# Splitting one 1280 KB weight load into four loads of 32 partitions, with another destination

## The chip, the cores and the metric

The kernel runs on one core of a Trainium2 chip. The metric is the device time of one execution in microseconds (us); the median of three runs stands for a kernel. All data is fp32.

## The reference, cut to what matters

The program is one decoder block for two sequences (B = 2) with one new token each (D = 512): a layer norm, attention over a long cache, a gated MLP beside it, and a residual.

```python
xn = _layernorm(x, axis=-1)                      # x: [2, 1, 512]
q = (xn @ wq)                                    # wq: [512, 4096] -> 32 heads of 128
scores = einsum("bhqd,bhkd->bhqk", q, k) * Dh**-0.5   # k_cache: [2, 8, 32768, 128]
o = einsum("bhqk,bhkd->bhqd", softmax(scores), v)     # v_cache: the same shape, 4 heads share a kv head
s = o @ wo                                       # wo: [4096, 512]
gate, up = xn @ W_gate, xn @ W_up                # [512, 1792] each
g = silu(((gate * (gate > 0)) * up) @ W_down)    # W_down: [1792, 512]
return x + s * g
```

The caches are 2 x 268 MB, the weights 28 MB together. Nearly all bytes are read once.

## The kernel before

**The ring.** All large data goes through three slots of 64 KB per partition (16384 floats, `slot`, L66): first wq in slot one, W_gate and W_up in slot two, W_down in slot three, then 64 tiles of k and v, then wo. A slot is loaded again once everything that reads it is done. All these loads are issued by SyncE through one helper (`load`, L69 and L70), so that every one of them has line 70 in the profile; they wait in one queue and the sixteen DMA engines take their packets from it in order, each engine at its own pace.

**wq.** A partition p of slot one holds four rows of wq, 4p to 4p + 3, of 4096 floats each: 64 KB, the whole slot. The load is in two parts. The first (128 x 13824 floats, 6912 KB, 55296 bytes per partition) brings all but the first 2560 floats (10 KB, `SHIFT`) of each partition and starts at the slot's beginning. The second brings those 128 pieces of 10 KB to the slot's end. Its source is written with an outer dimension of eight (`"(t a i) n -> i a t n"`, a = 8, t = 16): the piece of row group 8t + a goes to partition 16a + t, so that the pieces stand in another order of partitions than the rest of wq. The left operand of the products follows: `xnp` has four planes of the normalized x, one for each i, and a fifth plane (L170 to L177) in the order of the moved pieces.

**What follows, in the order of the code.** W_gate and W_up (3584 KB each, 28672 bytes per partition), W_down (3584 KB), then the k and v tiles (8192 KB each, 65536 bytes per partition).

**project_q (L180).** q for both sequences: eight column blocks of 512, four to a half; a half is sixteen matmuls of 128 x 512 (four row steps i by four blocks c, each block to its own 32 partitions of the result, L194). A product whose columns were moved reads the fifth plane. q is then turned into the form that the scores need (L203 to L227). `mlp_gu` (L238), `mlp_h` and `mlp_down` (L264) compute the MLP. The first k tile can be loaded when project_q has read slot one, the second when mlp_gu has read slot two, the first v tile when mlp_down has read slot three.

**The loop.** For each of sixteen pairs of sequence and kv head: two k tiles and two v tiles are loaded; VectorE transposes the k tile in place in blocks (L304), TensorE computes the scores (L315), the softmax follows (L344 to L382), TensorE multiplies with v (L391). At the end come wo in six pieces, the output product, and four small stores.

Of the kernel before, what the change touches and what calls it, by code (L numbers as in the profile page):

```python
# [8 lines left out]
F32 = mybir.dt.float32  # L9
# [4 lines left out]
P = 128  # L14
Q = 32
# [7 lines left out]
SHIFT = 2560  # L23
# [5 lines left out]
def kernel(  # L29
# [12 lines left out]
    nc = tc.nc  # L42
    B, HKV, SK, DH = kc.shape
    D = x.shape[2]
# [5 lines left out]
    NKC = D // P  # L50
    FC = F // 4
    FI = F // P
# [6 lines left out]
    const = ctx.enter_context(tc.tile_pool(name="const", bufs=1))  # L59
# [3 lines left out]
    SLOT = ROWS * DH  # L63
    KT, VT, PT = {}, {}, {}

    def slot(name):  # L66
        return ring.tile([P, SLOT], F32, tag="r", align_bytes=ALIGN, name=name)

    def load(dst, src):  # L69
        nc.sync.dma_start(dst, src)  # L70

    wqs = slot("wq")
    QN = wq.shape[1]
    load(wqs[:, : SLOT - SHIFT], wq.rearrange("(p i) n -> p (i n)", p=P)[:, SHIFT:])
    load(
        wqs[:, SLOT - SHIFT :],
        wq.rearrange("(t a i) n -> i a t n", a=8, i=NKC)[0, :, :, :SHIFT],
    )

    row = work.tile([P, 512], F32, tag="row", name="xp", bufs=3)  # L80
    xp = row[:32, :]
# [2 lines left out]
    nc.vector.memset(xy, 0.0)  # L84
    nc.scalar.dma_start(xp[:B, :], x.rearrange("b s d -> (b s) d"))

    gus = slot("gu")
    gut = gus[:, : 2 * NKC * F].rearrange("p (w i f) -> p w i f", w=2, i=NKC)
    for w, src in enumerate((wg, wu)):
        load(  # L90
            gus[:, w * NKC * F : (w + 1) * NKC * F],
            src.rearrange("(p i) f -> p (i f)", p=P),
        )
    wds = slot("wd")
    load(wds[:, : FI * D], wd.rearrange("(p i) d -> p (i d)", p=P))
    wdt = wds[:, : FI * D].rearrange("p (i d) -> p i d", i=FI)

    ident = const.tile([P, P], F32, name="ident")
# [8 lines left out]
    n = 1  # L107
# [5 lines left out]
    for s in range(NS):  # L113
# [39 lines left out]
    m_ps = ps_c.tile([P, 512], F32, name="m_ps")  # L153
# [6 lines left out]
    xc, sq = xc_row[:32, :], sq_row[:32, :]  # L160
# [5 lines left out]
    nc.scalar.activation(st[:, 3:4], st[:, 2:3], AF.Sqrt, bias=eps_t, scale=1.0 / D)  # L166
    nc.vector.reciprocal(st[:, 4:5], st[:, 3:4])
    nc.vector.tensor_scalar(xc, xc, st[:, 4:5], None, op0=ALU.mult)
    xnp = const.tile([P, NKC + 1, 32], F32, name="xnp")
    nc.vector.tensor_copy(  # L170
        sq[:, :P].rearrange("b (a t) -> b a t", a=8),
        xc.rearrange("b (t a i) -> b i a t", a=8, i=NKC)[:, 0],
    )
    xcol = xc.rearrange("b (p i) -> b i p", i=NKC)
    for i in range(NKC):
        nc.tensor.transpose(m_ps[:, i * 32 : (i + 1) * 32], xcol[:, i, :], ident[:32, :32])  # L176
    nc.tensor.transpose(m_ps[:, NKC * 32 : (NKC + 1) * 32], sq[:, :P], ident[:32, :32])  # L177
    nc.vector.tensor_copy(xnp.rearrange("p k m -> p (k m)"), m_ps[:, : (NKC + 1) * 32])

    def project_q():  # L180
        pick = ident.rearrange("p (c m) -> p c m", c=4)[:, :, :B]
        nq = 2 * REP * 4 * B
        spread = work.tile([P, 4, 4, Q], F32, tag="row", name="spread", bufs=3)
        for kb in range(4):
            nc.vector.tensor_copy(  # L185
                spread[:, :, kb, :], ident.rearrange("p (e l) -> p e l", e=4)
            )
        for half in range(2):
            pq = S[0][half]
            for i in range(NKC):  # L190
                for c in range(4):
                    n0 = (half * 4 + c) * 512
                    lo = i * QN + n0 - SHIFT
                    nc.tensor.matmul(  # L194
                        pq[32 * c : 32 * c + 32, :],
                        xnp[:, i if lo >= 0 else NKC, :],
                        wqs[:, lo % SLOT : lo % SLOT + 512],
                        start=(i == 0),
                        stop=(i == NKC - 1),
                    )  # L200
        for half in range(2):
            qs = work.tile([P, 512], F32, tag="row", name=f"qs_{half}", bufs=3)
            nc.vector.tensor_copy(qs, S[0][half])  # L203
            for h in range(REP):
                lo = (half * REP + h) * 4 * B
                nc.tensor.matmul(
                    m_ps[:, lo : lo + 4 * B],
                    qs[:, h * DH : (h + 1) * DH],
                    pick,
                    start=True,  # L210
                    stop=True,
                )
        turned = const.tile([P, nq], F32, name="turned")
        nc.vector.tensor_copy(turned, m_ps[:, :nq])
        for e in range(4):
            nc.tensor.matmul(
                pt_ps[:, e * nq : (e + 1) * nq],
                spread[:, e].rearrange("p k l -> p (k l)"),
                turned,
                start=True,  # L220
                stop=True,
            )
        qp = pt_ps[:, : 4 * nq].rearrange("p (e f h m) -> p f m e h", e=4, f=2, h=REP)
        for half in range(2):
            for kb in range(4):
                part = slice(Q * kb, Q * kb + Q)
                nc.vector.tensor_copy(  # L227
                    qt[part, half * 8 : half * 8 + 8, :, kb * REP : (kb + 1) * REP],
                    qp[part, half],
                )  # L230
# [168 lines left out]
    def finish_group(g):  # L399
# [11 lines left out]
        if b == B - 1:  # L411
            src = OS.pop(hk).rearrange("p b c (q i) -> p q (b c) i", q=4)
            for dq in range(4):
# [7 lines left out]
                )  # L421

    project_q()
    mlp_gu(0)
    mlp_gu(1)
# [3 lines left out]
    with tc.manual_schedule(engines=None):  # L429
# [23 lines left out]
        g, h = NG - 2, NG - 1  # L453
# [23 lines left out]
        i = 0  # L477
# [22 lines left out]
        for i in range(WO_WIDE):  # L500
            a = i % 4
# [4 lines left out]
                start=(i < 4),  # L506
                stop=(i >= WO_WIDE - 4),
# [4 lines left out]
        for c in range(4):  # L512
# [4 lines left out]
                start=False,  # L517
                stop=False,
# [40 lines left out]
```

## Time and profile before

| | |
|---|---|
| time, median of 3 runs (lowest to highest) | 1330.22 us (1328.72 to 1330.5) |
| time of the profiled execution | 1328.65 us |
| span of the profiled execution, first to last instruction | 1326.8 us |
| busy: PE / DVE / ACT | 839.5 / 677.2 / 49.5 us |
| read from memory | 564.67 MB, 426 GB/s over the span |

The page gives busy time by engine, the span in 40 equal slices with what the DMA engines moved in each, the queues, the chain of work that ended last, and the groups of instructions. DMA packets are counted where they start, so the rate of a short stretch scatters with how many large packets start in it; the share is the mean busy share of the sixteen DMA engines. Times inside the trace are us from the span's start.

### The profile page before, as it was taken

To read this page: it belongs to the slowest core of one execution; us is meant where nothing else is said; L and a number is where in the kernel's file an instruction comes from. 1 tells how busy PE (TensorE), PEld (TensorE's weight loads), DVE (VectorE), ACT (ScalarE), POOL (GpSimd) and SP (SyncE) were. 2 spreads that over 40 slices of the span, in tenths; PEclk is the share of its full clock that TensorE was granted. 3 is DMA by queue.
4 is the path that set the end of the run, shared out by engine and by line. 5 is a ranking of instruction groups with operands and counts; after the bars stand their busy time and mean duration, and the time that the engine had idled before them with its cause. 6 is when DMAs were issued, how large, how long until landed. Compare 5 with 4: busy or idle time off the path is not lost.

```text
span 1326.8 us, 10365 instructions
## 1 busy us (share of the span) xinstructions
PE 839.5 (63%) x4657; PEld 206.5 (16%) x4657; DVE 677.2 (51%) x574; ACT 49.5 (4%) x133; POOL 0.7 (0%) x6
## 2 busy tenths in 40 slices
PE   0746577574656757565685746677576657756775
PEld 0201112120111212111121201112021111201121
DVE  2256291835629183562918447291745719178620
ACT  0000000000000000000000000000000000000000
POOL 0000000000000000000000000000000000000000
PEclk9979789788979879787987969888887878978899
DMA  9999999999999999999999999999999999999997
GB/s 289 423 426 441 429 441 424 439 433 431 433 429 441 429 437 429 443 427 433 433 437 427 437 437 427 435 433 439 427 435 433 435 431 433 435 435 435 422 426 310
DMA packets 11016, 565.33 MB, mean 426 GB/s; under 512 B 1226, under 2 KB 1242, under 8 KB 1628
## 3 DMA queue, kind: packets, MB, share of 16 engines
q1 hardware_dynamic: 10944, 564.67, 99.2%
q8 instruction: 36, 0.59, 0.2%
q14 instruction: 8, 0.07, 0.0%
q10 hardware_dynamic: 28, 0.01, 0.0%
HBM read 564.67 MB, written 0.00 MB: 426 GB/s over the span
## 4 chain that ended last, share of the span: by engine, by line
DMA 52%; DVE 24%; PE 22%; issue 2%; ACT 0%; another core or an unknown queue 0%; ACTq 0%; SPq 0%; DVEq 0%
DMA k<-in_A_k_cache_dram 41%; DVE k L304 19%; PE o_ps L391 8%; DMA v<-in_A_v_cache_dram 6%; PE pt_ps L370 6%; PE s L315 5%; DMA wo<-in_A_wo_dram 3%; DMA wq<-in_A_wq_dram 3%; DVE mx L328 2%; DVE pt L374 2%; PE s L194 1%; PE s L238 1%; DVE mrow L354 0%; PE m_ps L378 0%; PE m_ps L357 0%
## 5 line engine op out<-in xcount | busy, mean ns | idle before, releaser
L315 PE MATMUL s<-k,qt 128*32 128x512 f32 x2048 | 460.0, 693 | 342.0 <-DVE k L304 341.9
L304 DVE STREAM_TRANSPOSE k<-k 128x2048 f32<-128x2048 f32 x256 | 567.0, 2279 | 169.8 <-DMA k<-in_A_k_cache_dram 163.0
L391 PE MATMUL o_ps<-v,pt 128*16 128x512 f32 x2048 | 229.9, 604 | 15.0 <-DMA v<-in_A_v_cache_dram 14.9
L315 PEld LDWEIGHTS s<-k,qt 128*32 128x32 f32 x2048 | 87.7, 122 | 710.0 <-DVE k L304 563.5
L403 DVE SCALAR_TENSOR_TENSOR os<-o_ps,rl,mask 128x512 f32<-128x512 f32 x16 | 12.0, 750 | 226.1 <-PE o_ps L391 226.1
L370 PE MATMUL pt_ps<-w,perm 128*128 128x512 f32 x128 | 84.7, 796 | 32.3 <-ACT w L367 17.9
L367 ACT ACTIVATE w<-s,nb 128x512 f32<-128x512 f32 x64 | 43.2, 686 | 1163.0 <-DVE nb L361 1160.9
L391 PEld LDWEIGHTS o_ps<-v,pt 128*16 128x16 f32 x2048 | 58.2, 98 | 171.5 <-issue 151.7
L328 DVE TENSOR_REDUCE mx<-s 128x1 f32<-128x512 f32 x64 | 42.7, 667 | 66.4 <-PE s L315 66.4
L374 DVE STREAM_TRANSPOSE pt<-pt_ps 128x512 f32<-128x512 f32 x32 | 22.9, 717 | 98.6 <-PE pt_ps L370 98.6
L370 PEld LDWEIGHTS pt_ps<-w,perm 128*128 128x128 f32 x128 | 26.9, 233 | 73.1 <-ACT w L367 39.1
L194 PE MATMUL s<-wq,xnp 128*32 128x512 f32 x64 | 8.7, 704 | 20.8 <-DMA wq<-in_A_wq_dram 20.8
L415 PE MATMUL ot_ps<-os,place 128*128 128x256 f32 x64 | 16.0, 392 | 7.0 <-DVE os L403 7.0
L203 DVE COPY qs<-s 128x512 f32<-128x512 f32 x2 | 1.4, 693 | 28.6 <-PE s L194 28.6
L378 PE MATMUL m_ps<-l,same 128*128 128x1 f32 x32 | 6.3, 267 | 13.5 <-DVE l L377 13.5
L345 PE MATMUL m_ps<-ident,m 128*1 128x128 f32 x16 | 4.3, 270 | 15.5 <-DVE m L344 15.5
L415 PEld LDWEIGHTS ot_ps<-os,place 128*128 128x128 f32 x64 | 11.5, 189 | 15.6 <-DVE os L403 14.4
L357 PE MATMUL m_ps<-negs,mrow 1*128 1x1 f32 x32 | 6.0, 256 | 11.7 <-DVE mrow L354 11.7
L367 ACT ACTIVATION_READ_ACCUMULATOR w<-s,nb 128x1 f32 x64 | 12.8, 201 | 0.0
L176 PE MATMUL m_ps<-ident,xc 32*128 32x32 f32 x4 | 0.7, 298 | 15.0 <-DVE spread L185 15.0
L378 PEld LDWEIGHTS m_ps<-l,same 128*128 128x128 f32 x32 | 5.0, 195 | 32.0 <-DVE l L377 32.0
L264 PE MATMUL m_ps<-wd,ht 128*32 128x512 f32 x28 | 6.3, 1006 | 5.3 <-DMA wd<-in_B_W_down_dram 5.3
(75 smaller groups left out, 81.7 us busy)
## 6 DMA issues: line engine op xcount, KB each, us to landing
v<-in_A_v_cache_dram SPq DMA_DIRECT2D x2, 4096.0 KB
wq<-in_A_wq_dram SPq DMA_DIRECT2D x1, 6912.0 KB, 19.9
wo<-in_A_wo_dram SPq DMA_DIRECT2D x1, 4096.0 KB
gu<-in_B_W_gate_dram SPq DMA_DIRECT2D x1, 3584.0 KB
gu<-in_B_W_up_dram SPq DMA_DIRECT2D x1, 3584.0 KB
wd<-in_B_W_down_dram SPq DMA_DIRECT2D x1, 3584.0 KB, 58.5
wo<-in_A_wo_dram SPq DMA_DIRECT2D x1, 2048.0 KB
wq<-in_A_wq_dram SPq DMA_DIRECT2D x1, 1280.0 KB
```

Source lines behind the costliest of these rows:

```text
L194: nc.tensor.matmul(pq[32 * c : 32 * c + 32, :], xnp[:, i if lo >= 0 else NKC, :], wqs[:, lo % SLOT : lo % SLOT + 512], start=(i == 0), sto ...
L238: nc.tensor.matmul(ps[32 * c : 32 * c + 32, :FC], xnp[:, i, :], gut[:, w, i, c * FC : (c + 1) * FC], start=(i == 0), stop=(i == NKC - 1),)
L304: nc.vector.transpose(KT[t][:, part], KT[t][:, part])
L315: nc.tensor.matmul(S[u][s][Q * c : Q * c + Q, :], qt[:, g, e, :], mov[:, s, c, e], start=(e == 0), stop=(e == 3),)
L328: nc.vector.reduce_max(MX[g][:, i : i + 1], S[u][s], axis=AX.X)
L367: nc.scalar.activation(w, S[u][s], AF.Exp, bias=nb, scale=SCALE, accum_out=LS[g][:, i : i + 1])
L370: nc.tensor.matmul(pt_ps, perm[:, s, :], w, start=(s == 0), stop=(s == NS - 1))
L374: nc.vector.transpose(pt.rearrange("p j m -> p (j m)"), pt_ps)
L378: nc.tensor.matmul(m_ps[:, 300:301], same.rearrange("p r h -> p (r h)"), l, start=True, stop=True)
L391: nc.tensor.matmul(o_ps[Q * a : Q * a + NC * REP], w[:, j, s * NC * REP : (s + 1) * NC * REP], v[:, s, j], start=(u == 0 and s == 0 and j ...
L403: nc.vector.scalar_tensor_tensor(OS[hk][:, b], o_ps, RL.pop(g), mask.unsqueeze(2).to_broadcast([P, NC, DH]), op0=ALU.mult, op1=ALU.mult,)
L415: nc.tensor.matmul(ot_ps.rearrange("p b c i -> p (b c) i"), place[:, lo : lo + P], src[:, dq], start=(hk == 0 and dq == 0), stop=(hk == HK ...
```

## The change

The 128 pieces of 10 KB are loaded by four loads of 32 partitions instead of one load of 128. The order in which the pieces are read is unchanged: load h has an outer dimension of eight (a) and an inner one of four (b), and reads row groups 32h + 8b + a; with 4h + b for t, that is 8t + a as before, for each a in the same order. What differs is where they are written. Loads 0 and 1 write partitions 0 to 31 and 32 to 63 of slot one's last 10 KB, loads 2 and 3 the same partitions of 10 KB in slot three behind W_down, which had been unused; a takes four consecutive partitions in each load. Partitions 64 to 127 get none.

The products follow: where one matmul over 128 partitions used the fifth plane, two over 64 partitions accumulate, from a plane each (`xnx`). This is so for the five column blocks that begin below column 2560, so that project_q has 69 matmuls, not 64. The order of VectorE's small copies and of the two transposes ahead of it changes with that.

```diff
-    wqs = slot("wq")
+    wqs, gus, wds = slot("wq"), slot("gu"), slot("wd")
     QN = wq.shape[1]
+    HP = P // 2
     load(wqs[:, : SLOT - SHIFT], wq.rearrange("(p i) n -> p (i n)", p=P)[:, SHIFT:])
-    load(
-        wqs[:, SLOT - SHIFT :],
-        wq.rearrange("(t a i) n -> i a t n", a=8, i=NKC)[0, :, :, :SHIFT],
-    )
+    blocks = wq.rearrange("(h b a i) n -> i h a b n", h=4, b=4, i=NKC)[0]
+    moved = (wqs[:HP, SLOT - SHIFT :], wds[:HP, FI * D : FI * D + SHIFT])
+    for h in range(4):
+        load(moved[h // 2][Q * (h % 2) : Q * (h % 2) + Q, :], blocks[h, :, :, :SHIFT])
...
-    xnp = const.tile([P, NKC + 1, 32], F32, name="xnp")
-    nc.vector.tensor_copy(
-        sq[:, :P].rearrange("b (a t) -> b a t", a=8),
-        xc.rearrange("b (t a i) -> b i a t", a=8, i=NKC)[:, 0],
-    )
+    xnp = const.tile([P, NKC, 32], F32, name="xnp")
+    xnx = const.tile([HP, 2, 32], F32, name="xnx")
+    for h in range(4):
+        nc.vector.tensor_copy(
+            sq[:, Q * h : Q * h + Q].rearrange("m (a b) -> m a b", a=8),
+            xc.rearrange("m (h b a i) -> m i h a b", h=4, b=4, i=NKC)[:, 0, h],
+        )
...
-    nc.tensor.transpose(m_ps[:, NKC * 32 : (NKC + 1) * 32], sq[:, :P], ident[:32, :32])
-    nc.vector.tensor_copy(xnp.rearrange("p k m -> p (k m)"), m_ps[:, : (NKC + 1) * 32])
+    for k in range(2):
+        nc.tensor.transpose(
+            m_ps[:HP, (NKC + k) * 32 : (NKC + k + 1) * 32],
+            sq[:, k * HP : k * HP + HP],
+            ident[:32, :32],
+        )
+    nc.vector.tensor_copy(xnp.rearrange("p k m -> p (k m)"), m_ps[:, : NKC * 32])
+    nc.vector.tensor_copy(
+        xnx.rearrange("p k m -> p (k m)"), m_ps[:HP, NKC * 32 : (NKC + 2) * 32]
+    )
...
-            for i in range(NKC):
+            steps = [[] for _ in range(4)]
+            for c in range(4):
+                n0 = (half * 4 + c) * 512
+                for i in range(NKC):
+                    lo = i * QN + n0 - SHIFT
+                    if lo >= 0:
+                        steps[c].append((xnp[:, i, :], wqs[:, lo : lo + 512]))
+                    else:
+                        for k in range(2):
+                            steps[c].append((xnx[:, k, :], moved[k][:, n0 : n0 + 512]))
+            for i in range(NKC + 1):
                 for c in range(4):
-                    n0 = (half * 4 + c) * 512
-                    lo = i * QN + n0 - SHIFT
-                    nc.tensor.matmul(
-                        pq[32 * c : 32 * c + 32, :],
-                        xnp[:, i if lo >= 0 else NKC, :],
-                        wqs[:, lo % SLOT : lo % SLOT + 512],
-                        start=(i == 0),
-                        stop=(i == NKC - 1),
-                    )
+                    if i < len(steps[c]):
+                        nc.tensor.matmul(
+                            pq[32 * c : 32 * c + 32, :],
+                            *steps[c][i],
+                            start=(i == 0),
+                            stop=(i == len(steps[c]) - 1),
+                        )
```

The first place is SyncE's queue at the program's start. A row is a load, tile and source by the program's names; DMAHW0 to DMAHW7 are eight counters that the loads use in turn and raise when they have landed, PE and DVE are counters of those engines. Before:

```order
L70 DMA wq<-in_A_wq_dram 128x13824
L70 DMA wq<-in_A_wq_dram 128x1x2560
L70 DMA gu<-in_B_W_gate_dram 128x7168
L70 DMA gu<-in_B_W_up_dram 128x7168
L70 DMA wd<-in_B_W_down_dram 128x7168
L70 DMA k_0_274<-in_A_k_cache_dram 128x16384 [waits DMAHW2_49,DMAHW0_49,PE_49]
```

After:

```order
L70 DMA wq<-in_A_wq_dram 128x13824
L70 DMA wq<-in_A_wq_dram 32x1x2560 x2
L70 DMA wd<-in_A_wq_dram 32x1x2560 x2
L70 DMA gu<-in_B_W_gate_dram 128x7168
L70 DMA gu<-in_B_W_up_dram 128x7168
L70 DMA wd<-in_B_W_down_dram 128x7168 [waits DMAHW0_49]
L70 DMA k_0_288<-in_A_k_cache_dram 128x16384 [waits DMAHW2_49,DMAHW3_49,DMAHW1_49,PE_49]
```

Three loads are added, and the counters come round sooner: the load of W_down, which waited for nothing, now waits for the counter of the first wq load. No load has changed its place against another.

The second place is TensorE's queue in project_q; s_0 is the first half's result and s_1 the second's. Before:

```order
L177 MATMUL m_ps<-ident,sq 128x32 [waits DVE_49]
L194 MATMUL s_0_120<-wq,xnp 32x512 [waits DMAHW2_49,DVE_49]
L194 MATMUL s_0_120<-wq,xnp 32x512 x3
L194 MATMUL s_0_120<-wq,xnp 32x512 [waits DMAHW0_49]
L194 MATMUL s_0_120<-wq,xnp 32x512 x11
L194 MATMUL s_1_121<-wq,xnp 32x512 x16
```

After:

```order
L179 MATMUL m_ps<-ident,sq 64x32 [waits DVE_49] x2
L212 MATMUL s_0_123<-wq,xnx 32x512 [waits DMAHW3_49,DMAHW2_49,DVE_49]
L212 MATMUL s_0_123<-wq,xnx 32x512 x3
L212 MATMUL s_1_124<-wq,xnx 32x512
L212 MATMUL s_1_124<-wq,xnp 32x512 [waits DMAHW0_49]
L212 MATMUL s_1_124<-wq,xnp 32x512 x2
L212 MATMUL s_0_123<-wd,xnx 32x512 [waits DMAHW5_49,DMAHW4_49]
L212 MATMUL s_0_123<-wd,xnx 32x512 x3
L212 MATMUL s_0_123<-wq,xnp 32x512 x12
L212 MATMUL s_1_124<-wd,xnx 32x512
L212 MATMUL s_1_124<-wq,xnp 32x512 x12
```

Eight matmuls that need only the first three loads have moved ahead of the wait for the last two; 29 stand behind it, where all 64 stood behind the wait for the second load.

More of the change, by code (lines that the diff above doesn't have):

```diff
@@ L85 @@
     nc.scalar.dma_start(xp[:B, :], x.rearrange("b s d -> (b s) d"))
-    gus = slot("gu")
     gut = gus[:, : 2 * NKC * F].rearrange("p (w i f) -> p w i f", w=2, i=NKC)
@@ L93 @@
         )
-    wds = slot("wd")
     load(wds[:, : FI * D], wd.rearrange("(p i) d -> p (i d)", p=P))
```

## The prediction

> **What bounds the kernel now.** I read the page first: its DMA rows, the HBM row, the queue, the chain.
>
> ```profile
> span 1326.8 us, 10365 instructions
> GB/s 289 423 426 441 429 441 424 439 433 431 433 429 441 429 437 429 443 427 433 433 437 427 437 437 427 435 433 439 427 435 433 435 431 433 435 435 435 422 426 310
> q1 hardware_dynamic: 10944, 564.67, 99.2%
> HBM read 564.67 MB, written 0.00 MB: 426 GB/s over the span
> DMA 52%; DVE 24%; PE 22%; issue 2%; ACT 0%; another core or an unknown queue 0%; ACTq 0%; SPq 0%; DVEq 0%
> ```
>
> One queue keeps the sixteen DMA engines busy 99.2% of the span, at about 433 GB/s in nearly every slice. The chain names DVE and PE for 46%, but while they work the queue does not run dry: packets are always waiting. So the kernel lasts as long as its bytes take, and the place to look is a slice that is slower. The first is: 289 GB/s over 33 us. The windows view cuts it up (last two columns: mean busy share of the DMA engines, and GB/s).
>
> ```profile
> 4.00:18.00 14.00, 0.76 (x5) 0.66 (x5) 6.88 (x32) 0.29 (x1) 0.00 (x0) 1.00 1.02 443
> 18.60:35.50 16.90, 0.00 (x0) 0.00 (x0) 0.00 (x0) 0.00 (x0) 0.00 (x0) 1.00 1.03 171
> 18.60:38.00 19.40, 1.37 (x8) 0.46 (x12) 0.00 (x0) 0.00 (x0) 0.00 (x0) 1.00 1.01 198
> 40.00:54.00 14.00, 12.99 (x116) 5.67 (x112) 5.16 (x13) 1.28 (x1) 0.00 (x0) 1.00 1.01 433
> 200.00:400.00 200.00, 127.69 (x715) 32.41 (x707) 94.29 (x81) 8.48 (x24) 0.00 (x0) 0.86 1.00 434
> 1309.00:1314.00 5.00, 2.69 (x16) 1.68 (x20) 1.32 (x4) 0.00 (x0) 0.00 (x0) 1.00 0.97 413
> ```
>
> The first wq load runs at 443 GB/s, W_gate to W_down later at 433. Between them lie 17 us in which all engines are busy and move 171. What runs there, the DMA view says by packets:
>
> ```profile
> DMA packets 206, 2.89 MB, mean 171 GB/s; under 512 B 23, under 2 KB 23, under 8 KB 23
> wq<-in_A_wq_dram SPq DMA_DIRECT2D x1, 1280.0 KB
> ```
>
> That is the answer for 18.6 to 35.5 us. 23 packets are completions; the other 183, of 10,240 and 28,672 bytes, make 2.89 MB if 128 are pieces of the second wq load and 55 belong to W_gate. So the second load fills this stretch, and W_gate's packets pass it on engines that have none of it. The code gives its source an outer dimension of eight; I take it that eight engines carry it (sixteen pieces each) and eight go on with W_gate. Then a piece takes 16.9 x 1.03 x 8 / 128 = 1.09 us and a W_gate packet 16.9 x 1.03 x 8 / 55 = 2.5 us, where an engine's share of the full rate, 443 / 16 = 27.7 GB/s, makes 0.37 and 1.04 us. Both kinds are slowed by 2.4 to 3 times, and nothing computes meanwhile (PE, DVE and ACT columns are zero).
>
> The price: 19.4 us from 18.6 to 38 at 198 GB/s are 3.84 MB, which at 433 GB/s take 8.87 us. **10.5 us are lost there.**
>
> **Why it is slow.** Small packets are not the cause: from 1309 to 1314 us the wo pieces move at 413 GB/s.
>
> ```profile
> DMA packets 182, 2.06 MB, mean 413 GB/s; under 512 B 18, under 2 KB 18, under 8 KB 30
> ```
>
> Its 164 packets of data average 12.5 KB. The source as such speaks little for it: the first load reads the same rows (55,296 of every 65,536 bytes) at 443. What is left is particular to the second load: an engine writes sixteen consecutive partitions (16a to 16a + 15), so that eight engines cover all 128, while the eight with W_gate write there too. In every stretch at full rate, each load covers 128 partitions over all sixteen engines, so an engine has its own eight. I take the slowness for engines meeting on the same destinations. It also explains why W_gate, at full rate later, suffers with it.
>
> The Trainium skill fits this to partitions ("DMA: Bandwidth & Descriptors", The descriptor swizzle): in a load of 128 partitions engine e of the first eight writes partitions 4e to 4e + 3 and the four 32 further on, and engines 8 to 15 do so from 64 up. By that, sixteen consecutive partitions lie in four engines' places, and half of them in those of the engines with W_gate; four loads of 32 keep engine a on its own. No row here shows a partition.
>
> **The change part by part.**
>
> *The four loads.* Same bytes, same order of reading, eight engines, each to four partitions per load, none to 64 and up. Bounds for this load: the 16.9 us it takes now, and half of the first load's rate, 1.31 MB / 221 GB/s = 5.9 us, when nobody is in the way. I take 5.9: a load by engines that keep to their own destinations is what the 443 and 433 rows show. W_gate beside it then runs at its 1.04 us per packet, and both groups gain the same 10.5 us. Eight engines keep 160 KB more to carry than the others, as now, so how far the groups stand apart (some 6 us) stays.
>
> *Where it lands.* The chain at the start:
>
> ```profile
> 1.20 35.30 DMA wq<-in_A_wq_dram
> 36.63 8.71 PE s L194 x64
> 52.26 0.96 another core or an unknown queue
> 53.27 3.26 PE s L238 x32
> ```
>
> wq is complete at 36.50 us, and should be at 26.0.
>
> *Three more loads on SyncE, and the wait of W_down's.* An issue costs SyncE about 0.5 us:
>
> ```profile
> 0.73 1.24 SPq L70 DMA_DIRECT2D wq<-in_A_wq_dram  x2
> 3.15 0.47 SPq L70 DMA_DIRECT2D wd<-in_B_W_down_dram  x1
> wq<-in_A_wq_dram SPq DMA_DIRECT2D x1, 6912.0 KB, 19.9
> ```
>
> 1.5 us more, under the first load's 17 us. W_down's load now waits for that first load, which lands 19.9 us after its issue, at about 20.6. It is wanted only when the faster engines have done W_gate and W_up: sixteen packets of 1.04 us after 18.6, at 35.3. So 14 us of cover; if it were gone, the queue would be empty for what is missing. Behind it on SyncE stands only the first k load, which has to wait for project_q anyway.
>
> *Five more matmuls, three more copies, one more transpose.* A pass of four matmuls takes 0.85 us at first:
>
> ```profile
> 36.63 8.71 PE L194 MATMUL s<-wq,xnp 128*32 128x512 f32 x64 [20.84 <-DMA wq<-in_A_wq_dram]
> 37.46 0.23 PEld L194 LDWEIGHTS s<-wq,xnp 128*32 128x32 f32 x4 [0.62 <-issue]
> 38.31 0.23 PEld L194 LDWEIGHTS s<-wq,xnp 128*32 128x32 f32 x4 [0.62 <-issue]
> 45.40 0.33 SPq L70 DMA_DIRECT2D k<-in_A_k_cache_dram  x1
> ```
>
> The mean is 8.71 / 16 = 0.54. Halves of 64 partitions have no row; between nothing (the wait is shorter by eight matmuls) and two passes of 0.85 they add at most 1.7 us, and I take 0.9, hidden. Cover: the k load goes out at 45.40 when project_q is done, and the engines want it when W_down's packets end, sixteen packets of W_up and W_down, 17 us, after W_gate; both move 10.5 us, and 7 us or more lie between. W_up's matmuls waited 0.96 us for their data after W_gate's were done, so that up to 0.9 is free there too, and what exceeds it delays only the second k load, one tile (8.39 MB / 433 = 19.4 us) ahead of need. The small copies lie before 17 us, wq lands at 26.
>
> *The end.* The chain there is DMA again:
>
> ```profile
> 1284.15 38.86 DMA wo<-in_A_wo_dram
> 1323.06 0.44 PE s L491 x8
> ```
>
> Bytes and loads after W_down are unchanged, the queue never ran dry between 40 and 1300 us, so all 10.5 us arrive: 1328.65 - 10.5 = 1318.15 for an execution like the profiled one. The median stands 1.57 above that one, so I expect **1319.7 us**. A measurement of this kernel tells 0.2% (2.7 us) from no change; 10.5 us is 0.8%.
>
> **Rivals.**
>
> *The reading is slow, not the writing.* At any moment eight engines read pieces 64 KB apart, in the first load they need not, and the order of reading is exactly kept. Then nothing changes: 16.9 us for the load, 1330.2 us. For it: nothing in the rows shows a partition. Against: W_gate reads consecutive rows and is slowed as much. Chance 0.06.
>
> *Halves do not run side by side.* The four loads reach only partitions 0 to 63. If W_gate had to wait for them, the others would idle 5.9 us, and the gain is 10.5 - 5.9 = 4.6 us: 1325.6 us. Against it: W_gate packets do pass the second load now. The Trainium skill ("SBUF — State Buffer", Can I just issue two DMAs to hit both halves?) says that two loads to the two halves serialize; the 55 packets above disagree for this queue. Chance 0.06.
>
> *Slower: the pieces of a load are dealt out singly.* If a load of 32 partitions gives neighbouring pieces to neighbouring engines rather than four running ones to each, four engines always write one engine's place, and eight move two places' rate, 2 x 27.7 = 55 GB/s: 1.31 MB in 23.7 us, 6.8 more than now, with these engines last to the end: 1337.0 us. It decides from the point where the last piece lands after 36.5 us. Against: the loads of 128 at 443 GB/s cannot be dealt so, or they would be slow too. Chance 0.05.
>
> **How the numbers follow.** The forecast has 0.83. Its own range: 10.5 +/- 0.6 for the two windows' edges and up to half a us of the matmuls, and +/- 0.9 for runs as they lie around their median (1328.72 to 1330.5): 1318.0 to 1322.0, which leaves the three rivals out, 0.17, and little more. Faster by over 0.2%: forecast and second rival, 0.89; within: 0.06; slower: 0.05.
>
> **What would show it.** Right: from 18.6 to 35 us the windows give about 433 GB/s instead of 171, PE's first matmul of project_q starts before 25 us and those on the last loads by 26.5, the first slice of 40 rises from 289 to about 400 GB/s, every later event comes 10 to 11 us sooner. The matmul estimate is wrong if the first k load's issue is later than 36. The forecast is wrong if the stretch stays at 171 (reading), if it has eight busy engines, a share of 0.5 (halves), or if W_gate is fast and wq lands after 36.5 (dealt singly).

## The result, and the profile after

The changed kernel takes 1318.03 us (median of five runs, 1317.82 to 1319.29), the kernel before 1330.32 us beside it (five runs, 1328.72 to 1330.5). The ratio is 0.9911, with a 95% interval of 0.9897 to 0.9926: 9.8 to 13.7 us. The profiled execution took 1319.29 us, its span 1317.5.

Single runs of each kernel fall on two steps some 1.3 us apart (before about 1328.9 or 1330.3, after about 1318.0 or 1319.4), so that the gain is 10.9 us step against step, while the medians, mostly upper step before and lower after, differ by 12.3, and the profiled runs, which cross the other way, by 9.4.

The page after, the lines that answer to those of before:

```profile
span 1317.5 us, 10398 instructions
GB/s 407 433 440 438 426 432 438 436 425 436 444 422 438 429 436 436 430 432 438 433 429 438 436 430 430 438 438 423 442 430 430 442 424 434 438 434 425 432 427 290
q1 hardware_dynamic: 10968, 564.67, 99.1%
HBM read 564.67 MB, written 0.00 MB: 429 GB/s over the span
DMA 49%; DVE 27%; PE 22%; issue 2%; ACT 0%; SPq 0%; ACTq 0%; DVEq 0%
```

The first slice went from 289 to 407 GB/s. The rest is as it was: the same megabytes, the same queue, busy for the same share of a span that is 9.3 us shorter. The windows view of the changed kernel, at the same places of the start (last two columns: share of the DMA engines, GB/s):

```profile
4.00:18.00 14.00, 0.76 (x6) 0.66 (x6) 7.18 (x36) 0.29 (x1) 0.00 (x0) 1.00 1.02 443
18.60:35.50 16.90, 12.86 (x54) 2.16 (x58) 0.69 (x1) 0.00 (x0) 0.00 (x0) 1.00 1.01 432
18.60:38.00 19.40, 15.36 (x76) 2.87 (x76) 0.75 (x2) 0.00 (x0) 0.00 (x0) 1.00 1.02 437
40.00:54.00 14.00, 9.43 (x80) 3.43 (x82) 5.75 (x14) 1.28 (x1) 0.00 (x0) 0.86 1.03 442
```

The slow stretch is gone: 432 where 171 stood, at the same busy share. An engine that is busy need not be moving much; the share of 1.0 read the same in both kernels, and only the GB/s beside it told them apart. The second change is in the PE column: project_q now runs inside this stretch. The DMA view of 18.6 to 35.5 us counts the packets:

```profile
DMA packets 401, 7.30 MB, mean 432 GB/s; under 512 B 64, under 2 KB 64, under 8 KB 64
```

Without 64 completions these are 337 packets of data; 128 pieces (1.31 MB) leave 209 packets of W_gate and W_up (5.99 MB), where 55 went in the same time before. In the single packet records of the trace each of the 128 pieces took 385 ns, and a packet of W_gate 1062 ns. Before, a piece took 1017 ns in the mean, and half of the pieces 1123 ns or more; W_gate's packets took 2.7 us in the mean.

A tile of the main loop, by its k transposes in the chain that ended last, is how a gain at the start is followed through the program. Before:

```profile
101.37 8.89 DVE k L304 x4
```

After, the chain at the start, and the same four transposes:

```profile
2.09 20.42 DMA wq<-in_A_wq_dram
22.64 15.24 PE s L212 x74
41.66 6.18 PE s L255 x62
91.02 8.89 DVE k L321 x4
```

101.37 to 91.02 is 10.35 us. By the packet records, counted off tile by tile, the first k tile ends 9.8 us sooner, and every tile after it up to 1150 us 10.4 to 11.0 us sooner.

### The profile page after: what moved, and what is told of

It reads as the page before. It is cut to its first block, busy times and chain, and to the rows that moved or that the text cites. A ratio compares the mean times of both kernels' runs of the same rounds, so it can differ in the third digit from the quotient of the medians.

```text
span 1317.5 us, 10398 instructions
## 1 busy us (share of the span) xinstructions
PE 845.6 (64%) x4668; PEld 206.5 (16%) x4668; DVE 677.5 (51%) x578; ACT 49.8 (4%) x133; POOL 0.7 (0%) x6
## 4 chain that ended last, share of the span: by engine, by line
DMA 49%; DVE 27%; PE 22%; issue 2%; ACT 0%; SPq 0%; ACTq 0%; DVEq 0%
DMA k<-in_A_k_cache_dram 44%; DVE k L321 22%; PE o_ps L408 8%; PE pt_ps L387 6%; PE s L332 5%; DMA wo<-in_A_wo_dram 3%; DVE mx L345 2%; DMA wq<-in_A_wq_dram 2%; DVE pt L391 2%; PE s L212 1%; PE s L255 1%; DVE mrow L371 0%; PE m_ps L374 0%; PE m_ps L395 0%; PE m_ps L362 0%
## 5 line engine op out<-in xcount | busy, mean ns | idle before, releaser
L408 PE MATMUL o_ps<-v,pt 128*16 128x512 f32 x2048 | 228.8, 602 | 13.7 <-DMA v<-in_A_v_cache_dram 13.6
L387 PE MATMUL pt_ps<-w,perm 128*128 128x512 f32 x128 | 88.5, 829 | 32.3 <-ACT w L384 17.9
```

Source lines behind the costliest of these rows:

```text
L387: nc.tensor.matmul(pt_ps, perm[:, s, :], w, start=(s == 0), stop=(s == NS - 1))
L408: nc.tensor.matmul(o_ps[Q * a : Q * a + NC * REP], w[:, j, s * NC * REP : (s + 1) * NC * REP], v[:, s, j], start=(u == 0 and s == 0 and j ...
```

## The experiments

The theory: engines are slow where they write to the same part of on-chip memory at once, and what the part is follows from the partition. Rivals: the reading is what was slow; or each engine must keep to the place that a load of 128 partitions gives it; or splitting the load helped by itself. A last group of kernels asks what the remaining skew between the two groups of engines costs.

### Reading or writing

**The old destination with another source** (edit of the kernel before). The second load writes as before, but reads 10 KB pieces that lie in a row in the k cache, a run of sixteen for each engine. The moved numbers of wq are left out, so that q is not the block's q in those columns.

```diff
-        wq.rearrange("(t a i) n -> i a t n", a=8, i=NKC)[0, :, :, :SHIFT],
+        kc[0, 0, : 8 * 340]
+        .rearrange("(a r) d -> a (r d)", a=8)[:, : 16 * SHIFT]
+        .rearrange("a (t n) -> a t n", n=SHIFT),
```

> The kernel before, with its one load of 128 partitions by eight engines (sixteen consecutive partitions each), but the pieces are read from the k cache, 174 KB apart for the engines and without a gap within an engine; q is computed from the wrong numbers in the moved columns. Theory (destinations): the stretch stays near 171 GB/s and the time at 1330 us. Rival (order of reading): the stretch rises to 430 GB/s and the time falls to about 1319 us.

1328.93 us (1328.54 to 1331.96, ten runs), ratio 1.0 [0.9991, 1.0009]. Its windows:

```profile
18.60:35.50 16.90, 0.00 (x0) 0.00 (x0) 0.00 (x0) 0.00 (x0) 0.00 (x0) 1.00 1.04 171
18.60:38.00 19.40, 1.21 (x8) 0.45 (x12) 0.00 (x0) 0.00 (x0) 0.00 (x0) 1.00 1.02 196
```

Another source, the same 171 GB/s. The reading is not what was slow. The time lies on the lower step where 1330 was expected.

**The new destinations with another order of reading** (edit of the changed kernel, the copies of x alike). By the pattern, neighbouring engines now read pieces 256 KB apart instead of 64 KB, and one engine's pieces lie 2 MB apart instead of 512 KB.

```diff
-    blocks = wq.rearrange("(h b a i) n -> i h a b n", h=4, b=4, i=NKC)[0]
+    blocks = wq.rearrange("(b a h i) n -> i h a b n", h=4, b=4, i=NKC)[0]
```

> The changed kernel's destinations with another order of reading: load h, engine a, piece b read row group 32b + 4a + h, so that engines read 256 KB apart and an engine's successive pieces lie 2 MB apart. Theory (destinations): nothing changes, the stretch stays at 430 to 443 GB/s and the time at 1318 us. Rival (order of reading): the stretch falls below 400 GB/s and the time rises by up to 12 us.

1319.26 us (1317.94 to 1319.36), ratio 0.9919 [0.9904, 0.9934]: the changed kernel's own times, on both its steps. The window:

```profile
18.60:35.50 16.90, 12.96 (x54) 2.17 (x58) 0.69 (x1) 0.00 (x0) 0.00 (x0) 1.00 1.01 436
```

From both sides: with the destination kept, the source changes nothing, and the other way round the order of reading changes nothing. What counts is the destination.

### Which destinations

**Each engine in its neighbour's place, and each in its own.** Two edits of the changed kernel: all four loads go to partitions 4 to 35, or all to 0 to 31, of four separate regions, so that engine a writes four partitions either beside those of the changed kernel or at them. Two memsets are added for the rows that the loads miss. The products then leave out most of the moved rows of wq, and q is not the block's q.

```diff
+    spare = wds[:HP, FI * D + SHIFT : FI * D + 3 * SHIFT]
+    nc.vector.memset(moved[0], 0.0)
+    nc.vector.memset(moved[1], 0.0)
+    places = (moved[0], moved[1], spare[:, :SHIFT], spare[:, SHIFT:])
     for h in range(4):
-        load(moved[h // 2][Q * (h % 2) : Q * (h % 2) + Q, :], blocks[h, :, :, :SHIFT])
+        load(places[h][4 : 4 + Q, :], blocks[h, :, :, :SHIFT])
```

> The changed kernel's four loads, all to partitions 4 to 35 (of four regions), so that every engine writes the four partitions that are its neighbour's in a load of 128, and no two engines meet; q is computed from a wrong set of moved rows, and two memsets of 64 partitions stand ahead of the loads. Theory (engines are slow only where two write the same place): as the same kernel at partitions 0 to 31, 1318 to 1320 us, a piece 0.385 us. Rival (an engine is slow wherever it leaves its own place): pieces of 0.6 us or more and a time of 1322 us or more.

1319.33 us (1317.85 to 1319.39), ratio 0.9922 [0.9907, 0.9937]. The window of partitions 4 to 35:

```profile
18.60:38.00 19.40, 16.65 (x96) 5.45 (x96) 1.61 (x3) 0.00 (x0) 0.00 (x0) 1.00 1.02 436
```

> The same with all four loads to partitions 0 to 31, each engine on its own four; q is computed from a wrong set of moved rows. Both theories: a piece 0.385 us, the time 1318 to 1320 us. It is the measure for the other.

1318.7 us (1317.9 to 1319.39), ratio 0.992 [0.9905, 0.9935]. The window of partitions 0 to 31:

```profile
18.60:38.00 19.40, 16.93 (x90) 4.93 (x90) 1.38 (x2) 0.00 (x0) 0.00 (x0) 1.00 1.02 437
```

Nothing is lost by moving each engine one place on; every piece took 385 ns in both. So an engine has no home that it must keep to.

**Four loads of 32, but over all 128 partitions** (edit of the kernel before; 64 records of matmuls as before, the fifth plane in the new order). Loads 0 and 1 write where the changed kernel's do, loads 2 and 3 go to partitions 64 to 127, where the other eight engines are writing W_gate.

```diff
-    load(
-        wqs[:, SLOT - SHIFT :],
-        wq.rearrange("(t a i) n -> i a t n", a=8, i=NKC)[0, :, :, :SHIFT],
-    )
+    blocks = wq.rearrange("(h b a i) n -> i h a b n", h=4, b=4, i=NKC)[0]
+    for h in range(4):
+        load(wqs[Q * h : Q * h + Q, SLOT - SHIFT :], blocks[h, :, :, :SHIFT])
```

> Four loads of 32 partitions as in the changed kernel, in the same order of reading, but loads 2 and 3 go to partitions 64 to 127 of slot one (64 matmuls, one operand of 128 partitions, as before). Theory (engines meet on the same destinations): loads 0 and 1 run at full rate (a piece 0.37 to 0.39 us), in loads 2 and 3 each of the eight engines shares its four partitions' place with one engine that carries W_gate, so that a piece takes 0.77 us and W_gate halves its rate: the stretch loses 8 x 0.385 = 3.1 us, the time is about 1321 us. Rival (slow reading, by the order of the source): the load is as in the changed kernel or before, 1318 or 1330 us. Rival (only the number of loads matters): 1318 us.

1322.27 us (1321.27 to 1322.46), ratio 0.9943 [0.9928, 0.9958]. The windows, first while loads 0 and 1 run, then in loads 2 and 3, then the whole stretch:

```profile
18.60:21.60 3.00, 0.00 (x0) 0.00 (x0) 0.00 (x0) 0.00 (x0) 0.00 (x0) 1.00 1.02 434
22.00:28.00 6.00, 0.00 (x0) 0.00 (x0) 0.00 (x0) 0.00 (x0) 0.00 (x0) 1.00 1.09 254
18.60:38.00 19.40, 9.09 (x63) 2.65 (x64) 0.69 (x1) 0.00 (x0) 0.00 (x0) 1.00 1.02 372
```

One kernel shows both cases. As long as the eight engines stay below partition 64, the rate is 434; when they cross to where the others write, it falls to 254. In the packet records 72 pieces took 385 ns, most of the other 56 took 760 to 816, and W_gate's packets there some 2.1 us: two engines at one place take twice as long each. On its lower step the kernel took 1321.27 us, near the 1321 of the theory; both rivals are out. Splitting the load without keeping to the lower half brought some 8 us (1330.3 to 1322.4, step against step), keeping to it brought the last 3.

**Two loads of 64 partitions, all below 64** (edit of the changed kernel, the copies of x alike). Each engine gets eight consecutive partitions, so that engines a and a + 4 write to partitions 32 apart, and nobody goes to 64 and up.

```diff
-    blocks = wq.rearrange("(h b a i) n -> i h a b n", h=4, b=4, i=NKC)[0]
+    blocks = wq.rearrange("(h b a i) n -> i h a b n", h=2, b=8, i=NKC)[0]
...
-    for h in range(4):
-        load(moved[h // 2][Q * (h % 2) : Q * (h % 2) + Q, :], blocks[h, :, :, :SHIFT])
+    for h in range(2):
+        load(moved[h], blocks[h, :, :, :SHIFT])
```

> Two loads of 64 partitions instead of four of 32, both still on partitions 0 to 63: an engine writes eight consecutive partitions, so that engines a and a + 4 meet on the same place, and none meets an engine that carries W_gate. Theory (meeting on destinations): a piece takes 0.77 us, the load 12.3 us instead of 6.2, W_gate beside it stays at full speed; the eight engines come 6.2 us later than in the changed kernel, which is about 1324 us. Rival (what matters is that no piece goes to partitions 64 to 127): as the changed kernel, 1318 us.

1324.38 us (1323.67 to 1325.01), ratio 0.9958 [0.9942, 0.9975]. The time is as expected, the way to it is not. Windows, then the DMA view of 20 to 28 us:

```profile
20.00:28.00 8.00, 2.41 (x9) 0.58 (x10) 0.00 (x0) 0.00 (x0) 0.00 (x0) 1.00 1.01 229
18.60:38.00 19.40, 10.14 (x48) 1.92 (x48) 0.42 (x1) 0.00 (x0) 0.00 (x0) 1.00 1.02 314
```

```profile
DMA packets 129, 1.83 MB, mean 229 GB/s; under 512 B 8, under 2 KB 8, under 8 KB 8
```

129 packets less 8 completions are 121; 1.83 MB makes 89 of them pieces and 32 of them W_gate's. Eight engines in 8 us at a share of 1.01: 64.6 / 89 = 0.73 us for a piece, 64.6 / 32 = 2.0 us for a packet of W_gate. The pieces were expected to double, and did (median of all 128 in the packet records 773 ns). W_gate's packets were expected at full speed, since their engines meet nobody, and they doubled too. So, if W_gate's engines write from 64 up as the kernel before this one showed, slowness spreads from engines that meet to engines that don't.

Both kernels agree with the pairing in the Trainium skill ("DMA: Bandwidth & Descriptors", The descriptor swizzle): partitions 32 apart belong to one engine's place, those from 64 up to other engines'. By it a meets a + 4 here, and loads 2 and 3 of the kernel before this one meet W_gate's engines. That the pieces of this kernel are slow because a meets a + 4 rests on the page alone: that a run of eight partitions is slow by itself was not tried. For the spreading, the same page (Back-pressure in remote DMA) says of transfers between cores that a full destination also clogs engines that share its path. That would fit 2.0 us, but no run here shows a path.

### What the skew costs

**No moved pieces** (edit of the kernel before): wq comes as one load of 128 partitions, and all engines carry the same bytes.

```diff
-SHIFT = 2560
+SHIFT = 0
-    load(
-        wqs[:, SLOT - SHIFT :],
-        wq.rearrange("(t a i) n -> i a t n", a=8, i=NKC)[0, :, :, :SHIFT],
-    )
...
-xnp = const.tile([P, NKC + 1, 32], F32, name="xnp")
+xnp = const.tile([P, NKC, 32], F32, name="xnp")
...
```

> The kernel before with no moved pieces: wq in one load of 128 partitions over sixteen engines. Theory (the end is set by three engines that carry 160 KB more and fetches of instructions besides, 5 to 6 us after the other thirteen): 160 KB less on eight engines and 80 KB more on each of the sixteen take 3 us from those three, 1315 us. Rival (the slow stretch was all there was to win, and the skew between the two groups is of no account): 1318 us. Second rival (the skew keeps loads from ending together and is worth something by itself): 1320 us or more.

1316.72 us (1316.62 to 1316.82), ratio 0.9905 [0.9889, 0.9922]. Once more, on another chip:

> The kernel without moved pieces again, beside the changed kernel on the same chip. Theory (the nine engines that fetch instructions end last, and those of them with the pieces 5 us after the rest): 1316.7 us, 1.3 us or more ahead of the changed kernel. Rival (the difference between the earlier jobs is that of chips): equal.

1316.73 us (1316.65 to 1316.88), ratio 0.9901 [0.9885, 0.9918]. On that chip the changed kernel ran once more beside it:

> The changed kernel again: single runs fall on 1317.9 to 1318.2 or on 1319.3 us, a step of about 1.3 us, as those of the kernel before fall on 1328.7 to 1329.0 or 1330.1 to 1330.5.

1319.37 us (1319.26 to 1319.53), ratio 0.9921 [0.9906, 0.9936]. So the moved pieces cost the changed kernel 2.6 us on that chip, and 1.3 where it runs on its lower step. The expectation of 1315 asked for 3 us under the changed kernel's 1318: against that step about half of it came. The last 6 us of wo's loads show why. Each row is one window; the second last number is the share of the sixteen engines. Before, after, and without moved pieces:

```profile
1317.00:1323.00 6.00, 4.16 (x56) 1.05 (x56) 0.69 (x1) 0.00 (x0) 0.00 (x0) 1.00 0.23 93
```

```profile
1307.00:1313.00 6.00, 4.46 (x52) 0.84 (x44) 0.47 (x1) 0.00 (x0) 0.00 (x0) 1.00 0.18 72
```

```profile
1304.00:1310.00 6.00, 4.81 (x50) 0.86 (x46) 0.34 (x1) 0.00 (x0) 0.00 (x0) 1.00 0.50 204
```

In before and after some three or four of sixteen engines carry the end (0.23 x 16 = 3.7, 0.18 x 16 = 2.9); the others are done. Without moved pieces half of them work to the end. The packet records say who is late. The page after counts them in a queue of their own, and those of the other two have the same rows:

```profile
q8 instruction: 36, 0.59, 0.2%
q14 instruction: 8, 0.07, 0.0%
```

These packets fetch instructions. Where each data packet is joined to the one that starts as it ends, the records of the changed kernel's profiled run fall into a chain for each engine: the 36 of 16 KB fall on eight engines, four or five on each, and each costs its engine about 1.4 us (0.9 in which it moves no data, 0.5 by which its next packet is longer). A ninth engine loses 0.84 us five times to packets of 8 KB. Six of the nine are engines without moved pieces, where the loss eats into their lead; three have the moved pieces as well and end last. So there is skew without moved pieces too, and part of the moved pieces' skew is balanced by it.

One such loss is about as long as the step between single runs, and the traces fit that. The two engines that carry both the pieces and 16 KB fetches end last. They carry four fetches each in the three profiled runs on the lower step (before, the old destination with another source, partitions 0 to 31), and five each in the four on the upper one (the changed kernel twice, the other order of reading, partitions 4 to 35). With partitions 0 to 31 the last two engines end at 1314.8 us, with 4 to 35 at 1316.3, and the next one at 1310.5 and 1310.8. Why a run has one or the other is open.

**Smaller pieces** (edits of the changed kernel): 1024 floats are moved instead of 2560, then 512.

```diff
-SHIFT = 2560
+SHIFT = 1024
```

> The changed kernel with pieces of 4 KB instead of 10 KB (1024 columns; 67 matmuls). Theory (the end is set by three of the eight engines with the pieces): 98 KB less on these and 49 KB more on every engine take 1.8 us from the last three, 1316.2 us. Rivals: 1318 us (skew of no account), or 1319 us and more (skew worth something).

1316.92 us (1316.04 to 1317.61), ratio 0.9906 [0.9892, 0.9921]: nearer to the theory's 1316.2 than to the rivals, with single runs on two steps again (about 1316.2 and 1317.6).

> Pieces of 2 KB (512 columns, 66 matmuls). Theory: between the kernels without pieces and with 4 KB, 1316.5 to 1317 us, no better than without, since the three last engines gain 1.2 us at most against 4 KB and the others that fetch instructions lose as much. Rival (some skew is best): below 1316 us.

1315.88 us (1315.82 to 1316.88), ratio 0.9896 [0.9882, 0.9911], on the chip of the last two. With 512 the lowest median of all, 3.5 us under the changed kernel and 0.85 us under the one without moved pieces. The rival, that some skew is best, called for under 1316 and got it. But one of its four runs lies at 1316.88, where the other's highest lies, and the two intervals overlap: that 512 beats 0 is likely and not settled. Every run of either lies below every run of the changed kernel (1317.82 and up).

## Why the prediction was right, step by step

The forecast was 1319.7 us in a range of 1318.0 to 1322.0, and 1318.03 came, 0.03 us above the range's lower end. Two of the five runs lie below it, and on another chip four runs of the same kernel gave 1319.26 to 1319.53. The two margins named, 0.6 and 0.9, reach down to 1318.2 only. That this median fell inside was luck; the mechanism and the size of the gain were not.

**The stretch and its price: shown.** 171 GB/s became 432, and from 18.6 to 38 us 198 became 437: (437 - 198) x 19.4 / 433 = 10.7 us where 10.5 were forecast, and 10.9 arrive step against step.

**The cause: shown, but told too narrowly.** Engines that meet on destinations are what was slow, as the kernel over all 128 partitions shows in one run; the old destinations keep 171 GB/s with another source. The prediction held that W_gate suffered because its engines are met. The two loads of 64 show that it suffers as much when they aren't.

**The second load's 5.9 us, and W_gate's 1.04:** a piece took 385 ns, sixteen of them 6.2 us; a packet of W_gate 1.06. Both as priced.

**wq complete at 26.0: shown by the packets.** The last piece's packet ends at 25.2 us; before, it ended at 35.7, 0.8 us ahead of the 36.50 there, so that 26.0 fits. Of the two starts of matmuls that were to show it, one fits. SyncE's and TensorE's timelines of the changed kernel (start, duration, then what the engine did; in brackets what it waited for):

```profile
19.52 0.33 SPq L70 DMA_DIRECT2D wd<-in_B_W_down_dram  x1
37.94 10.25 SPq L70 DMA_DIRECT2D k<-in_A_k_cache_dram  x2
```

```profile
22.64 3.59 PE L212 MATMUL s<-wq,xnx 64*32 64x512 f32 x10 [6.82 <-DMA wq<-in_A_wq_dram]
26.16 1.93 PE L212 MATMUL s<-wq,xnp 128*32 128x512 f32 x6
28.02 1.93 PE L212 MATMUL s<-wd,xnx 64*32 64x512 f32 x8
29.88 4.32 PE L212 MATMUL s<-wq,xnp 128*32 128x512 f32 x24
34.12 1.04 PE L212 MATMUL s<-wd,xnx 64*32 64x512 f32 x2
35.10 2.78 PE L212 MATMUL s<-wq,xnp 128*32 128x512 f32 x24
37.81 1.39 PE L223 MATMUL m_ps<-ident,qs 128*128 128x8 f32 x11
```

project_q begins at 22.64, "before 25"; the matmuls on the last two loads begin at 28.02, not "by 26.5". No wait stands in front of them, so it was TensorE that was late, not the data.

**Three more issues, and W_down's wait: as costed.** W_down's load goes out at 19.52, when the first wq load has landed, a little ahead of the 20.6 forecast and 15.8 us ahead of the 35.3 at which it is wanted.

**The matmul term: mis-sized.** Forecast +0.9 us, 1.7 at most, and "wrong if the first k load's issue is later than 36". It came at 37.94, 7.5 us sooner than the 45.40 of before and not 10 to 11, and project_q took 15.24 us for 8.71: +6.5. Three things went into this. First the count. The trace keeps two records for each of these matmuls, so that the 64 records before are 32 matmuls, and 37 issued after (74 records), not 64 and 69 as the text on the change has it; pieces of 1024 and 512 columns make 34 and 33, not 67 and 66. Second, the passes. Matmuls share a pass if they stand four abreast, one for each column block; those of the fifth block stand alone and take whole passes. Read off the records' starts, two records to a matmul, the ten, six, eight, 24, two and 24 records are 4 + 2 + 2 + 6 + 2 + 6 = 22 passes, where there were 16. Third, their speed. Before, four passes took some 0.84 us and most of the rest 0.43; after, the first eleven take 0.83 to 1.01, 0.89 in the mean, until 32.4 us, and the other eleven 0.49 in the mean: 11 x 0.89 + 11 x 0.49 = 15.2 us.

The excess was hidden all the same. project_q had begun 3.5 us ahead of the 26.1 that a wait for all of wq would have meant, so that the k load was only some 2 us later than forecast; and the faster engines, with 24 packets of 1.06 us each after 18.6, come to it at 44.0 (the first k packet starts at 44.3), 6 us after its issue. The window from 40 to 54 us shows 442 GB/s: the queue did not run dry.

**All of it arrives at the end: shown**, 10.35 us in the chain at 91 us, 10.4 to 11.0 in the loads up to 1150 us, 10.9 in the times. **The skew of some 6 us stays: shown** by the windows of the tail, though part of it is the instruction fetches'. **The 1.57 us between profiled execution and median** was added as if after would fall on the steps as before did; its runs fell mostly on the lower one. This is why 1318.0 came and not 1319.7; the four runs on the other chip, all on the upper step, gave 1319.37.

**The rivals.** The reading: refuted by the old destination with another source. The halves one after the other: refuted by 432 GB/s over the whole stretch, at which the Trainium skill's rule ("SBUF — State Buffer", Can I just issue two DMAs to hit both halves?) doesn't hold for a load on eight engines with one of 128 partitions behind it in the queue. Pieces dealt singly: refuted by the same rate, and by 385 ns for each piece.

## What to carry to other kernels

Where a load does not cover all partitions the usual way, work out which engine writes which partitions at the same time as the others; two engines at one place halve each other, and here also those beside them, though all show as busy. Read GB/s beside the busy share, and look for the stretch in which they part. And check the cover of a cheap extra matmul rather than its price: this one's was wrong by a factor of seven and cost nothing.

## What the runs showed of the hardware

- Pieces of 10 KB took 385 ns where no two engines met, mostly 760 to 820 where two did, and 1017 in the mean, half of them 1123 or more, in the kernel before, whose engines each run over sixteen consecutive partitions.
- Engines that, by the reading above, meet nobody are slowed along: 2.0 us instead of 1.06 for a packet of W_gate in the kernel with two loads of 64. By which way is open.
- Eight of sixteen engines lose about 1.4 us to each of four or five instruction fetches, 5.6 to 7 us over the program, and a ninth some 4 us to smaller ones. This decides with the loads' shapes which engines end last.
- The half-speed start of a run of matmuls can last. With PEclk at 1.00 in the window, passes took 0.83 to 1.01 us for some 10 us in the changed kernel, and some 0.84 us for 3.4 us before. In the kernel without moved pieces project_q also starts at 22.8 us, but with full passes only. Its timeline:

```profile
22.77 9.36 PE L185 MATMUL s<-wq,xnp 128*32 128x512 f32 x64 [5.97 <-DMA wq<-in_A_wq_dram]
```

The 9.36 us there are near the 8.71 of before, so the early start is not what made the passes slow for so long. The Trainium skill ("TensorE: Matmul & The Clock Gate", Part 1: The HAM clock gate) gives about 3.4 us of sustained work until full speed. The kernel before agrees with its 3.4 us; the changed one, six of whose 22 passes hold fewer than four matmuls, doesn't. The other traces point to those passes: the slow start lasts 3.4 to 5.1 us in the five kernels whose passes are all full, and 8 to 11 us in the seven that have partly filled ones and no wait between them. No run changes the passes alone, so the reason stays open.
